# Larger reads for the MLP's first weight, a split last K pair, z1 products in the waits of z2, and the output store on another queue

## The chip, the cores and the metric

The kernel runs on one core of one Trainium2 chip. The metric is the device time of one execution in microseconds (us), lower is better. The profile's "span" of an execution is from its first to its last recorded instruction; it is 1.7 to 2.1 us shorter than the device time of the same execution in most cases, and up to 3.0 us shorter in about one of seven.

## The reference

One decode step: attention over the last 4,096 keys of 32 heads of 192, then a gated MLP. All data are bf16.

```python
# x: [1,1,640]; caches [1,32,32768,192]; wq [640,6144]; wo [6144,640]; w_in [640,1536]; w_out [768,640]
def _A_ref(x, k_cache, v_cache, wq, wo):
    q = (x @ wq) split into 32 heads
    k, v = k_cache[:, :, Sk - 4096:], v_cache[:, :, Sk - 4096:]
    p = softmax(q @ k.T * 192 ** -0.5)
    return (p @ v) @ wo
def _B_ref(x, w_in, w_sp, b_sp, w_out):
    z = gelu(x @ w_in)                    # 1,536 columns
    z1 = z[..., :768]
    z2 = layernorm(z[..., 768:])
    g = w_sp * z2 + b_sp                  # S is 1: two scalars
    return (z1 * g) @ w_out
h = x + _A_ref(layernorm(x), ...)
out = h + _B_ref(layernorm(h), ...)
```

The caches are 100.7 MB of the 119.3 MB that have to be read. w_in is 1.97 MB and w_out 0.98 MB; they are needed last, after the attention.

## The kernel before

All large loads are issued from one list by one engine (SP), in the order in which they are wanted, and wait only for buffers. Heads are worked through in 16 pairs `t`. The end of the list, and how w_in is read:

```python
win_v = B_w_in.rearrange("(c p) f -> p c f", p=P)      # c: 5 chunks of 128 rows
LAST = (0, J // 2, 3 * J // 4, 7 * J // 8, J)
def dma_pair(kind, cache, t_):                         # K or V of one head pair, 3 MB
    cuts = LAST if t_ == NP - 1 else (0, J)            # the last pair lands in four pieces
    ...
plan.append(("wo", lambda: dma_wo(NQ - 1)))
for f0 in (Fh, 0):                                     # columns 768.. (z2) first, then 0.. (z1)
    for a, b in ((0, 3), (3, DC)):
        plan.append(("w", lambda f0=f0, a=a, b=b: load(w_in_sb[:, a:b, f0:f0 + Fh], win_v[:, a:b, f0:f0 + Fh])))
for c in range(FHC):
    plan.append(("w", lambda c=c: load(w_out_sb[:, c, :], wout_v[c])))
```

So z2's half of w_in is wholly read before z1's half, in rows of 768 columns, which are packets of 1,536 bytes. The tail that consumes them:

```python
    # ... h_pc, mean and rstd2 of the layernorm of h; hb1 = h - mean
    def half_in(f0):                                   # 30 products: 5 chunks c, 6 column blocks
        zv = bank()
        for c in range(DC):
            for fb in range(FHC):
                nc.tensor.matmul(zv[:, fb:fb + 1], lhsT=w_in_sb[:, c, f0 + fb * P:...], rhs=hb1[:, c:c + 1], ...)
        return zv[:, 0:FHC]
    z2_ps = half_in(Fh)
    nc.scalar.activation(out=T3[:, 0:FHC], in_=z2_ps, func=ACT.Gelu_apprx_tanh, scale=rstd2, accum_out=sums3[:, 0:1])
    nc.vector.scalar_tensor_tensor(out=tsq[:], ...)    # the squares, and their sum
    # 16 products that put h into orow, then:
    nc.tensor.matmul(lin_ps, lhsT=rootF_f[:], rhs=sums3[:], start=True, stop=True)
    # ... VectorE and ScalarE: layernorm of z2, gz = w_sp * z2 + b_sp
    z1_ps = half_in(0)
    nc.scalar.activation(out=z1[:], in_=z1_ps, func=ACT.Gelu_apprx_tanh, scale=rstd2)
    nc.vector.tensor_tensor(out=gv[:], in0=z1[:], in1=gz[:], op=ALU.mult)
    for c in range(FHC):                               # 24 w_out products
        for g in range(NG):
            nc.tensor.matmul(orow[32 * g:32 * g + 1, :], lhsT=gv[:, c:c + 1], rhs=w_out_sb[:, c, g * OW:(g + 1) * OW], ...)
    nc.vector.tensor_copy(out=o_sb[:], in_=orow)
    nc.sync.dma_start(out=out[0, 0].rearrange("(g n) -> g n", g=NG), in_=o_sb[0::32, :])
```

Of the kernel before, what the change touches and what calls it, by code (L numbers as in the profile page):

```python
# [16 lines left out]
def kernel(  # L17
# [14 lines left out]
    nc = tc.nc  # L32
    P = nc.NUM_PARTITIONS
# [4 lines left out]
    J = W // HALF  # L38
    DC = D // P
    HD = H * Dh  # L40
    F = B_w_in.shape[-1]
    Fh = F // 2
    FC = F // P
    FHC = Fh // P
    NP = H // 2
# [10 lines left out]
    NE16 = 32  # L56

    def load(out, in_):
        eng = nc.sync
        eng.add_instruction(mybir.InstDMACopy(  # L60
            name=nc.get_next_instruction_name(), mode="Copy", queue="qSPDynamicHW",
            ins=eng.lower_ap_dma(in_, for_custom_bir_dma=True),
            outs=eng.lower_ap_dma(out, for_custom_bir_dma=True)))

    def pair_keys(cache, t, a, b):
        h0 = 4 * (t // 2) + t % 2
        k0 = Sk - W + a * HALF
        return cache[0, h0:h0 + 3:2, k0:k0 + (b - a) * HALF, :].rearrange("h (p j) d -> p h (j d)", p=HALF // 2)

    RQ = 4 * Dh // P  # L70
    NQ = NP // 2
    wo_v = A_wo.rearrange("(q e i) n -> q e (i n)", q=NQ, e=NE16)
    win_v = B_w_in.rearrange("(c p) f -> p c f", p=P)
    wout_v = B_w_out.rearrange("(c e i) n -> c e (i n)", c=FHC, e=NE16)
    wq_v = A_wq.rearrange("(c p i) n -> c p (i n)", c=DC, i=4)
    LAST = (0, J // 2, 3 * J // 4, 7 * J // 8, J)
# [15 lines left out]
    def bank():  # L92
        return psum.tile([P, 512], F32, tag="sm", name="sm_ps", bufs=3)
# [5 lines left out]
    x_row = const.tile([1, D], BF16)  # L99
    w_in_sb = wp.tile([P, DC, F], BF16)  # L100
    w_out_sb = wp.tile([P, FHC, D], BF16)

    def dma_wq(i):
        t = kvp.tile([P, KVE], BF16, tag="kv", name="wq_t")
        for c in range(2 * i, min(2 * i + 2, DC)):
            load(t[:, (c % 2) * HD:(c % 2 + 1) * HD], wq_v[c])
        tiles[("wq", i)] = t

    def dma_pair(kind, cache, t_):
        t = kvp.tile([P, KVE], BF16, tag="kv", name=kind + "_t")  # L110
        cuts = LAST if t_ == NP - 1 else (0, J)
        for a, b in zip(cuts, cuts[1:]):
            load(t[:, None, a * Dh:b * Dh], pair_keys(cache, t_, a, b))
        tiles[(kind, t_)] = t

    def dma_wo(q):
        t = wop.tile([P, RQ * D], BF16, tag="wo", name="wo_t")
        if q < NQ - 1:
            load(t[:], wo_v[q])
        else:  # L120
            rows_v = A_wo.rearrange("(q p i) n -> q p (i n)", q=NQ, p=P)[q]
            for a in range(0, RQ, RQ // 2):
                load(t[:, a * D:(a + RQ // 2) * D], rows_v[:, a * D:(a + RQ // 2) * D])
        tiles[("wo", q)] = t

    plan = [("kv", lambda i=i: dma_wq(i)) for i in range(NWQ)]
    for t_ in range(2):
        plan.append(("kv", lambda t=t_: dma_pair("k", A_k_cache, t)))
    for t_ in range(NP):
        if t_ + 2 < NP:  # L130
            plan.append(("kv", lambda t=t_ + 2: dma_pair("k", A_k_cache, t)))
        if t_ % 2 == 1 and t_ < NP - 1:
            plan.append(("wo", lambda q=t_ // 2: dma_wo(q)))
        plan.append(("kv", lambda t=t_: dma_pair("v", A_v_cache, t)))
    plan.append(("wo", lambda: dma_wo(NQ - 1)))
    for f0 in (Fh, 0):
        for a, b in ((0, 3), (3, DC)):
            plan.append(("w", lambda f0=f0, a=a, b=b: load(w_in_sb[:, a:b, f0:f0 + Fh], win_v[:, a:b, f0:f0 + Fh])))
    for c in range(FHC):
        plan.append(("w", lambda c=c: load(w_out_sb[:, c, :], wout_v[c])))  # L140
    limit = {"kv": KVB, "wo": WOB, "w": DC + FHC}
# [7 lines left out]
    def free(kind, n=1):  # L149
        live[kind] -= n  # L150
        issue()
# [10 lines left out]
    ones_bf = const.tile([P, P], BF16)  # L162
# [7 lines left out]
    rootF_f = const.tile([P, P], F32)  # L170
# [32 lines left out]
    for h_ in range(2):  # L203
        id_h = ident_f[:, 64 * h_:64 * h_ + 64].rearrange("p (g c) -> p c g", g=2)
        for k_ in range(8):
            c0 = 2 * (k_ * (h_ + 1) // 2)
# [52 lines left out]
    for gq in range(0, NQ, 4):  # L259
        for w0 in range(0, 2 * Dh, P):  # L260
            psv = sc_bank()[:].rearrange("p (q w) -> p q w", q=4)
            for c in range(DC):
                wc = wq_sb[c // 2][:, (c % 2) * HD:(c % 2 + 1) * HD].rearrange("p (q a w) -> p q a w", q=NQ, a=2)
                for a in range(2):
                    nc.tensor.matmul(psv, lhsT=xn2[:, c, a, :], rhs=wc[:, gq:gq + 4, a, w0:w0 + P],  # L265
                                     start=(c == 0 and a == 0), stop=(c == DC - 1 and a == 1))
# [9 lines left out]
    attn_ps = psum.tile([P, 512], F32, tag="acc", name="attn_ps", bufs=1)  # L276
    DH2 = D // 2
    rows = attn_ps[:, DC + 3:DC + 3 + DH2]
# [133 lines left out]
    def project(q, oT):  # L412
        wo_t = tiles.pop(("wo", q))
        o = small.tile([P, RQ], BF16, tag="o6", name="o6")
        rz = rzq.pop(q)
        if q < NQ - 1:
            o2v = oT[:, 0:2 * RQ].rearrange("p (i a) -> p a i", a=2)
            o0 = small.tile([P, RQ], F32, tag="o0", name="o0")
            nc.vector.tensor_scalar(out=o0[:], in0=o2v[:, 0], scalar1=rz[:, 0:1], scalar2=None, op0=ALU.mult)
            nc.vector.scalar_tensor_tensor(out=o[:], in0=o2v[:, 1], scalar=rz[:, 1:2], in1=o0[:], op0=ALU.mult, op1=ALU.add)  # L420
        else:
            nc.vector.tensor_scalar(out=o[:], in0=oT[:, 0:RQ], scalar1=rz[:, 0:1], scalar2=None, op0=ALU.mult)
        for i in range(RQ):
            if q < NR:
                for h_ in range(2):
                    p0 = 32 * (i % 2) + 64 * h_
                    c0 = i * D + h_ * DH2
                    nc.tensor.matmul(rows[p0:p0 + 1, :], lhsT=o[:, i:i + 1], rhs=wo_t[:, c0:c0 + DH2],  # L428
                                     start=(q == 0 and i < 2), stop=(q == NR - 1 and i >= RQ - 2))
            else:  # L430
                for nb in range(DC):
                    nc.tensor.matmul(attn_ps[:, nb:nb + 1], lhsT=wo_t[:, i * D + nb * P:i * D + (nb + 1) * P],
                                     rhs=o[:, i:i + 1], start=False,
                                     stop=(q == NQ - 1 and i == RQ - 1 and nb == DC - 1))
        free("wo")

    def fold(rows_sb):
        for c in range(DC):
            nc.tensor.matmul(attn_ps[:, c:c + 1], lhsT=x_row[0:1, c * P:(c + 1) * P], rhs=ones_bf[0:1, 0:1],
                             start=(c == 0), stop=False)  # L440
        for c in range(DC):
            for h_ in range(2):
                lo, hi = max(c * P, h_ * DH2), min((c + 1) * P, (h_ + 1) * DH2)
                if lo < hi:
                    nc.tensor.matmul(attn_ps[lo - c * P:hi - c * P, c:c + 1],
                                     lhsT=rows_sb[:, lo - h_ * DH2:hi - h_ * DH2], rhs=halfsel[:, h_:h_ + 1],
                                     start=False, stop=False)

    NR = NQ - 2
    assert NCH == 2  # L450
    for t in range(NP):
# [24 lines left out]
        if q_on:  # L476
            project((t - 5) // 2, oT)
# [22 lines left out]
    NG = 4  # L500
# [27 lines left out]
    nc.vector.tensor_tensor(out=hv2[:], in0=mh[:], in1=half_ps, op=ALU.subtract)  # L528
    rstd2 = ln_rstd(hv2)

    def half_in(f0):
        zv = bank()
        for c in range(DC):
            for fb in range(FHC):
                nc.tensor.matmul(zv[:, fb:fb + 1], lhsT=w_in_sb[:, c, f0 + fb * P:f0 + (fb + 1) * P], rhs=hb1[:, c:c + 1],
                                 start=(c == 0 and fb == 0), stop=(c == DC - 1 and fb == FHC - 1))
        return zv[:, 0:FHC]

    z2_ps = half_in(Fh)
    sums3 = const.tile([P, 2], F32)  # L540
    nc.scalar.activation(out=T3[:, 0:FHC], in_=z2_ps, func=ACT.Gelu_apprx_tanh, scale=rstd2, accum_out=sums3[:, 0:1])
    tsq = small.tile([P, FHC + 1], F32, tag="tsq", name="tsq", bufs=1)
    nc.vector.scalar_tensor_tensor(out=tsq[:], in0=T3[:], scalar=0.5 ** 0.5, in1=T3[:], op0=ALU.mult, op1=ALU.mult,
                                   accum_out=sums3[:, 1:2])
    for g in range(NG):
        for c in range(DC):
            lo, hi = max(g * OW, c * P), min((g + 1) * OW, (c + 1) * P)
            if lo < hi:
                nc.tensor.matmul(orow[32 * g:32 * g + 1, lo - g * OW:hi - g * OW], lhsT=h_pc[:, c:c + 1],
                                 rhs=ident_f[:, lo - c * P:hi - c * P], start=(lo == g * OW), stop=False)  # L550
    lin_ps = bank()[:, 0:2]
    nc.tensor.matmul(lin_ps, lhsT=rootF_f[:], rhs=sums3[:], start=True, stop=True)
    m3 = small.tile([P, 2], F32, tag="lnm", name="lnm")
    nc.vector.tensor_copy(out=m3[:], in_=lin_ps)
    hv3 = small.tile([P, 1], F32, tag="lnv", name="lnv")
# [6 lines left out]
    rstd3 = ln_rstd(hv3)  # L562
    gz = small.tile([P, FHC], F32, tag="gz", name="gz", bufs=1)
    nc.vector.tensor_scalar(out=gz[:], in0=Tw[:], scalar1=rstd3, scalar2=sp_f[:, 1:2], op0=ALU.mult, op1=ALU.add)
    z1_ps = half_in(0)
    z1 = small.tile([P, FHC], F32, tag="z1", name="z1", bufs=1)
    nc.scalar.activation(out=z1[:], in_=z1_ps, func=ACT.Gelu_apprx_tanh, scale=rstd2)
    gv = small.tile([P, FHC], BF16, tag="gv", name="gv", bufs=1)
# [1 line left out]
    for c in range(FHC):  # L570
        for g in range(NG):
            nc.tensor.matmul(orow[32 * g:32 * g + 1, :], lhsT=gv[:, c:c + 1], rhs=w_out_sb[:, c, g * OW:(g + 1) * OW],
                             start=False, stop=(c == FHC - 1))
    o_sb = small.tile([P, OW], BF16, tag="o_sb", name="o_sb", bufs=1)
    nc.vector.tensor_copy(out=o_sb[:], in_=orow)
    nc.sync.dma_start(out=out[0, 0].rearrange("(g n) -> g n", g=NG), in_=o_sb[0::32, :])

_INS = ['A_x', 'A_k_cache', 'A_v_cache', 'A_wq', 'A_wo', 'B_x', 'B_w_in', 'B_w_sp', 'B_b_sp', 'B_w_out']
_OUTS = [((1, 1, 640), 'bfloat16')]
# [24 lines left out]
```

## Time and profile before

| | before |
|---|---|
| device time, median of 6 runs | 288.17 us (287.54 to 288.41) |
| span of the profiled execution | 285.5 us |
| read | 119.34 MB, 418 GB/s over the span |
| last w_out packet has landed (packet records) | 281.72 us |
| last product starts / o_sb done / span ends | 282.18 / 282.87 / 285.5 us |

The page of before. The second and third lines cut the span into 40 slices (busy tenths of the 16 DMA engines, and what they moved); a "q" line is a DMA queue with its packets, megabytes and share of 16 engines' span; the last line sums the chain of work that ended last.

```profile
span 285.5 us, 3043 instructions
...
DMA  8999999999999999999999999999999999999992
GB/s 331 399 434 441 434 434 402 435 461 441 429 441 413 434 406 441 430 460 441 441 409 407 434 441 435 440 458 413 441 425 403 441 441 410 467 441 396 394 401 103
...
q1 hardware_dynamic: 5544, 119.35, 97.5%
q8 instruction: 9, 0.15, 0.2%
q14 instruction: 4, 0.03, 0.0%
...
DMA 67%; PE 16%; DVE 14%; SPq 1%; issue 1%; DVEq 0%
...
```

The DMA engines are busy until the last slice, and two thirds of the chain are waits for them. The row "q8 instruction" is nine packets of 16 KB with which the core fetched instructions (each is called a "fetch").

The timeline of before's tail. The columns are start (us), duration, engine, line, operation, output<-inputs, shapes and count; brackets hold idle time of the engine before the group and what ended it.

```profile
...
274.18 0.44 PEld L432 LDWEIGHTS <-wo_t 128*128 128x128 bf16 x15 [0.15 <-DMA wo_t<-in_A_wo_dram]
...
275.79 0.62 PE L535 MATMUL sm_ps<-hb_1930,w_in_sb 128*128 128x1 bf16 x18
...
276.59 0.48 PE L535 MATMUL sm_ps<-hb_1930,w_in_sb 128*128 128x1 bf16 x12 [0.18 <-DMA w_in_sb<-in_B_w_in_dram]
...
278.88 0.64 PE L535 MATMUL sm_ps<-hb_1930,w_in_sb 128*128 128x1 bf16 x18 [0.38 <-DMA w_in_sb<-in_B_w_in_dram]
...
279.82 0.48 PE L535 MATMUL sm_ps<-hb_1930,w_in_sb 128*128 128x1 bf16 x12 [0.30 <-DMA w_in_sb<-in_B_w_in_dram]
...
280.63 0.17 DVE L569 TENSOR_TENSOR gv<-z_2042,gz 128x6 bf16<-128x6 f32 x1 [0.19 <-ACT z_2042 L567]
...
280.86 1.63 PE L572 MATMUL sc_ps<-w_out_sb,gv 128*1 128x160 bf16 x24 [0.56 <-DVE gv L569]
...
282.54 0.33 DVE L575 CAST o_sb<-sc_ps 128x160 bf16<-128x160 f32 x1 [1.74 <-PE sc_ps L572]
...
```

The 18 and 12 products of L535 are z2's chunks 0 to 2 and 3 to 4, then the same for z1. The second group of z2 starts 2.41 us after the last piece of wo_t was seen (274.18 to 276.59). The 24 w_out products take 1.63 us because they wait for w_out's arrivals. The chain of waits says the same (start, duration, what):

```profile
...
264.50 12.05 DMA w_in_sb<-in_B_w_in_dram
...
276.56 5.58 DMA w_out_sb<-in_B_w_out_dram
...
282.18 0.33 PE sc_ps L572 x4
...
282.54 0.33 DVE o_sb L575
...
```

The last thing before the four last products is a DMA: when this execution ends is set by the arrival of w_out.

### The profile page before, as it was taken

The page shows a single profiled execution, that of the slowest core. Times are in us where ns is not written, and L with a number is a line of the kernel's source. Part 1 is how long each engine was busy: PE and PEld are TensorE (multiplying, and loading weights), DVE is VectorE, ACT ScalarE, POOL GpSimd, SP SyncE. Part 2 cuts the span into 40 slices and gives each one's busy share as a digit, 9 for nine tenths or more (in the row PEclk, how much of TensorE's full clock was granted, in tenths as well). Part 3 has the DMA queues.
Part 4 walks back from the last instruction along what each step waited for, and adds up shares of the span by engine and source line. Part 5 has one row for each costly group of instructions (what it writes and reads, how often), then busy time and mean ns, then how long its engine had stood idle before and what let it go on. Part 6 is the DMA issues. An engine that isn't in the chain of part 4 may idle for free.

```text
span 285.5 us, 3043 instructions
## 1 busy us (share of the span) xinstructions
PE 188.1 (66%) x1245; PEld 77.6 (27%) x1245; DVE 193.3 (68%) x282; ACT 26.4 (9%) x98; POOL 2.3 (1%) x10
## 2 busy tenths in 40 slices
PE   1229947778764665935593775756972787778873
PEld 0003413223222221312131222222321222334562
DVE  7300098989994948688595939595786849984632
ACT  2001200101102010201002010201010010202311
POOL 3000000000000000000000000000000000000000
PEclk9999989799999698979979879967797759987675
DMA  8999999999999999999999999999999999999992
GB/s 331 399 434 441 434 434 402 435 461 441 429 441 413 434 406 441 430 460 441 441 409 407 434 441 435 440 458 413 441 425 403 441 441 410 467 441 396 394 401 103
DMA packets 5563, 119.53 MB, mean 419 GB/s; under 512 B 1005, under 2 KB 2286, under 8 KB 2990
## 3 DMA queue, kind: packets, MB, share of 16 engines
q1 hardware_dynamic: 5544, 119.35, 97.5%
q8 instruction: 9, 0.15, 0.2%
q14 instruction: 4, 0.03, 0.0%
q10 hardware_dynamic: 6, 0.00, 0.0%
HBM read 119.34 MB, written 0.00 MB: 418 GB/s over the span
## 4 chain that ended last, share of the span: by engine, by line
DMA 67%; PE 16%; DVE 14%; SPq 1%; issue 1%; DVEq 0%
DMA k_t<-in_A_k_cache_dram 35%; DMA v_t<-in_A_v_cache_dram 19%; PE sc_ps L299 9%; DVE k_t L293 9%; DMA wq_t<-in_A_wq_dram 7%; PE sc_ps L265 5%; DMA w_in_sb<-in_B_w_in_dram 4%; DMA w_out_sb<-in_B_w_out_dram 2%; DVE ob L395 1%; DVE S L307 1%; SPq L60 1%; PE pv_169 L370 1%; PE attn_ps L428 1%; PE sm_ps L317 0%; DVE gm L319 0%
## 5 line engine op out<-in xcount | busy, mean ns | idle before, releaser
L299 PE MATMUL sc_ps<-k_t,ident_bf 128*128 128x512 bf16 x384 | 112.3, 455 | 43.8 <-DVE k_t L293 43.8
L293 DVE TENSOR_TENSOR k_t<-k_t,q_203 128x6144 bf16<-128x6144 bf16 x32 | 107.2, 3353 | 36.7 <-DMA k_t<-in_A_k_cache_dram 36.7
L299 PEld LDWEIGHTS <-ident_bf 128*128 128x128 bf16 x384 | 41.8, 113 | 104.6 <-issue 65.5
L265 PE MATMUL sc_ps<-wq_t,xn_128 128*128 128x512 bf16 x60 | 17.7, 455 | 10.8 <-DMA wq_t<-in_A_wq_dram 8.4
L307 DVE TENSOR_REDUCE S<-sc_ps 128x32 f32<-128x512 f32 x32 | 21.8, 682 | 2.0 <-PE sc_ps L299 2.0
L273 DVE COPY sp_f<-sm_ps 128x2 f32<-128x2 f32 x1 | 0.2, 160 | 25.9 <-PE sm_ps L271 25.9
L265 PEld LDWEIGHTS <-xn_128 128*128 128x128 bf16 x60 | 6.5, 110 | 21.6 <-issue 14.2
L332 ACT ACTIVATE E_125<-S,bias 128x64 bf16<-128x64 f32 x12 | 4.2, 360 | 73.8 <-DVE bias L326 73.8
L319 DVE TENSOR_REDUCE gm<-sm_ps 2x1 f32<-2x128 f32 x16 | 4.5, 279 | 8.4 <-PE sm_ps L317 8.4
L332 ACT ACTIVATE E_126<-S,bias 128x64 bf16<-128x64 f32 x10 | 3.5, 361 | 68.2 <-DVE bias L326 68.2
L332 ACT ACTIVATE E_127<-S,bias 128x64 bf16<-128x64 f32 x10 | 3.5, 362 | 67.1 <-DVE bias L326 67.1
L370 PE MATMUL pv_171<-v_t,E_126 128*8 128x512 bf16 (+1 forms) x72 | 7.1, 458 | 2.7 <-DMA v_t<-in_A_v_cache_dram 2.7
L370 PE MATMUL pv_169<-v_t,E_127 128*8 128x512 bf16 (+1 forms) x72 | 7.1, 457 | 0.5 <-DMA v_t<-in_A_v_cache_dram 0.5
L267 ACT ACTIVATE q_203<-sc_ps 128x512 bf16<-128x512 f32 x6 | 3.6, 597 | 29.3 <-PE sc_ps L265 29.3
L370 PE MATMUL pv_169<-v_t,E_125 128*8 128x512 bf16 (+1 forms) x72 | 6.2, 424 | 0.0
L370 PEld LDWEIGHTS <-E_126 128*8 128x8 bf16 (+1 forms) x120 | 3.4, 89 | 8.1 <-issue 5.4
L370 PEld LDWEIGHTS <-E_127 128*8 128x8 bf16 (+1 forms) x120 | 3.5, 86 | 7.1 <-issue 4.7
L370 PE MATMUL pv_171<-v_t,E_127 128*8 128x512 bf16 (+1 forms) x48 | 4.2, 425 | 1.8 <-DMA v_t<-in_A_v_cache_dram 1.8
L370 PE MATMUL pv_171<-v_t,E_125 128*8 128x512 bf16 (+1 forms) x48 | 4.2, 425 | 1.5 <-DMA v_t<-in_A_v_cache_dram 1.5
L370 PEld LDWEIGHTS <-E_125 128*8 128x8 bf16 (+1 forms) x120 | 3.2, 84 | 6.7 <-issue 4.0
L370 PE MATMUL pv_169<-v_t,E_126 128*8 128x512 bf16 (+1 forms) x48 | 4.2, 423 | 0.0
L324 PEld LDWEIGHTS sm_ps<-ident_f,gm 2*128 2x128 f32 x16 | 2.0, 128 | 7.4 <-issue 5.7
(225 smaller groups left out, 141.3 us busy)
## 6 DMA issues: line engine op xcount, KB each, us to landing
k_t<-in_A_k_cache_dram SPq DMA_DIRECT2D x15, 3072.0 KB, 32.0
v_t<-in_A_v_cache_dram SPq DMA_DIRECT2D x15, 3072.0 KB, 32.1
wq_t<-in_A_wq_dram SPq DMA_DIRECT2D x5, 1536.0 KB, 14.2
wo_t<-in_A_wo_dram SPq DMA_DIRECT2D x7, 960.0 KB, 20.5
k_t<-in_A_k_cache_dram SPq DMA_DIRECT2D x1, 1536.0 KB
v_t<-in_A_v_cache_dram SPq DMA_DIRECT2D x1, 1536.0 KB
w_in_sb<-in_B_w_in_dram SPq DMA_DIRECT2D x2, 576.0 KB, 14.0
wo_t<-in_A_wo_dram SPq DMA_DIRECT2D x2, 480.0 KB, 13.0
```

Of the source, the lines that this page charges most:

```text
L60: eng.add_instruction(mybir.InstDMACopy(name=nc.get_next_instruction_name(), mode="Copy", queue="qSPDynamicHW", ins=eng.lower_ap_dma(in_, ...
L265: nc.tensor.matmul(psv, lhsT=xn2[:, c, a, :], rhs=wc[:, gq:gq + 4, a, w0:w0 + P], start=(c == 0 and a == 0), stop=(c == DC - 1 and a == 1))
L267: nc.scalar.activation(out=q2f[:, gq:gq + 4, w0:w0 + P], in_=psv, func=ACT.Copy, scale=scale)
L293: nc.vector.tensor_tensor(out=kc, in0=kc, in1=q2[:, t:t + 1, :].to_broadcast([P, JC, Dh]), op=ALU.mult)
L299: nc.tensor.matmul(psv, lhsT=ident_bf[:], rhs=k3[:, ch * JC:(ch + 1) * JC, n * G:(n + 1) * G], start=(n == 0), stop=(n == NT - 1))
L307: nc.vector.tensor_reduce(out=S[:, ch * JC:(ch + 1) * JC], in_=st[t]["ps"][ch], axis=AX.X, op=ALU.add)
L319: nc.vector.tensor_reduce(out=gm[:], in_=mT[0:2, 0:P], axis=AX.X, op=ALU.max)
L324: nc.tensor.transpose(out=nb[:, 0:2], in_=gm[:].to_broadcast([2, P]), identity=ident_f[0:2, 0:2])
L332: nc.scalar.activation(out=E[:, :, a], in_=S[:], func=ACT.Exp, bias=bias[:, a:a + 1], accum_out=zq[q][:, a, b:b + 1])
L370: nc.tensor.matmul(pv[p0:p0 + 2 * n, :].rearrange("p (k r i) -> p k r i", k=n, r=32), lhsT=E[:, j0:j0 + n, :].rearrange("p j a -> p (j a)" ...
L395: nc.vector.tensor_reduce(out=ob[:, i0:i0 + ni], in_=flat.rearrange("p (k r i) -> p i r k", k=n, i=ni), axis=AX.X, op=ALU.add)
L428: nc.tensor.matmul(rows[p0:p0 + 1, :], lhsT=o[:, i:i + 1], rhs=wo_t[:, c0:c0 + DH2], start=(q == 0 and i < 2), stop=(q == NR - 1 and i >= ...
```

## The change

Its intent: fewer and larger packets for w_in, so that the loads end earlier; a finer last step and less work in the tail; z1's first products in time in which TensorE waits anyway; and an output store that does not use SP. Rows 0 to 383 of w_in are read whole (12,288 bytes a packet), so both halves of these rows come before z2's rows 384 to 639.

```diff
+    win_rows = B_w_in.rearrange("(c e i) f -> c e (i f)", c=DC, e=NE16)
+    WHOLE = 3
-        cuts = LAST if t_ == NP - 1 else (0, J)
+        cuts = (0, J) if t_ < NP - 1 else LAST if kind == "v" else (0, J // 2, J)
+    for c in range(WHOLE):
+        plan.append(("w", lambda c=c: load(w_in_sb[:, c, :], win_rows[c])))
     for f0 in (Fh, 0):
-        for a, b in ((0, 3), (3, DC)):
-            plan.append(("w", lambda f0=f0, a=a, b=b: load(w_in_sb[:, a:b, f0:f0 + Fh], win_v[:, a:b, f0:f0 + Fh])))
+        plan.append(("w", lambda f0=f0: load(w_in_sb[:, WHOLE:, f0:f0 + Fh], win_v[:, WHOLE:, f0:f0 + Fh])))
 ...  # x's products: 5 in the fold (the attention's rows turned into columns, near the end) become 2 in the first projection
-    z2_ps = half_in(Fh)
+    part_in(z2_ps, Fh, 0, DC)
+    part_in(z1_ps, 0, 0, WHOLE)          # z1's 18 products for rows 0 to 383
     nc.scalar.activation(out=T3[:, 0:FHC], in_=z2_ps, func=ACT.Gelu_apprx_tanh, ...)
 ...
+    nc.tensor.matmul(lin_ps, lhsT=rootF_f[:], rhs=sums3[:], start=True, stop=True)   # before h's 16 products
 ...
-    nc.tensor.matmul(lin_ps, lhsT=rootF_f[:], rhs=sums3[:], start=True, stop=True)   # was after them
 ...
-    z1_ps = half_in(0)
+    part_in(z1_ps, 0, WHOLE, DC)         # z1's other 12 products
 ...
-    nc.sync.dma_start(out=out[0, 0].rearrange("(g n) -> g n", g=NG), in_=o_sb[0::32, :])
+    nc.scalar.dma_start(out=out[0, 0].rearrange("(g n) -> g n", g=NG), in_=o_sb[0::32, :])
```

More of the change, by code (lines that the diff above doesn't have):

```diff
@@ L422, in project @@
             nc.vector.tensor_scalar(out=o[:], in0=oT[:, 0:RQ], scalar1=rz[:, 0:1], scalar2=None, op0=ALU.mult)
+        if q == 0:
+            for h_ in range(2):
+                nc.tensor.matmul(rows[64 * h_:64 * h_ + 1, :], lhsT=ones_bf[0:1, 0:1], rhs=x_row[0:1, h_ * DH2:(h_ + 1) * DH2],
+                                 start=True, stop=False)
         for i in range(RQ):
@@ L428, in project @@
                     nc.tensor.matmul(rows[p0:p0 + 1, :], lhsT=o[:, i:i + 1], rhs=wo_t[:, c0:c0 + DH2],
-                                     start=(q == 0 and i < 2), stop=(q == NR - 1 and i >= RQ - 2))
+                                     start=(q == 0 and i == 1), stop=(q == NR - 1 and i >= RQ - 2))
             else:
@@ L438, in fold @@
         for c in range(DC):
-            nc.tensor.matmul(attn_ps[:, c:c + 1], lhsT=x_row[0:1, c * P:(c + 1) * P], rhs=ones_bf[0:1, 0:1],
-                             start=(c == 0), stop=False)
-        for c in range(DC):
             for h_ in range(2):
@@ L446, in fold @@
                                      lhsT=rows_sb[:, lo - h_ * DH2:hi - h_ * DH2], rhs=halfsel[:, h_:h_ + 1],
-                                     start=False, stop=False)
+                                     start=(c == 0), stop=False)
     NR = NQ - 2
@@ L529, with part_in @@
     rstd2 = ln_rstd(hv2)
-    def half_in(f0):
-        zv = bank()
-        for c in range(DC):
+    def part_in(zv, f0, c0, c1):
+        for c in range(c0, c1):
             for fb in range(FHC):
@@ L536, in half_in @@
                                  start=(c == 0 and fb == 0), stop=(c == DC - 1 and fb == FHC - 1))
-        return zv[:, 0:FHC]
-    z2_ps = half_in(Fh)
+    z2_ps = bank()[:, 0:FHC]
+    part_in(z2_ps, Fh, 0, DC)
+    z1_ps = bank()[:, 0:FHC]
+    part_in(z1_ps, 0, 0, WHOLE)
     sums3 = const.tile([P, 2], F32)
@@ L544 @@
                                    accum_out=sums3[:, 1:2])
+    lin_ps = bank()[:, 0:2]
+    nc.tensor.matmul(lin_ps, lhsT=rootF_f[:], rhs=sums3[:], start=True, stop=True)
     for g in range(NG):
@@ L550 @@
                                  rhs=ident_f[:, lo - c * P:hi - c * P], start=(lo == g * OW), stop=False)
-    lin_ps = bank()[:, 0:2]
-    nc.tensor.matmul(lin_ps, lhsT=rootF_f[:], rhs=sums3[:], start=True, stop=True)
     m3 = small.tile([P, 2], F32, tag="lnm", name="lnm")
```

## The prediction

> **What bounds the kernel now.** DMA, to the end. The page: 119.3 MB at 418 GB/s over 285.5 us; its slice table has the DMA share at 9 tenths until the last slice; 67% of the chain of waits is DMA, its last pieces v_t (29.2 us), w_in_sb (12.1), w_out_sb (5.6). The trace's packet records show each DMA engine reading nearly without gaps from 2.1 us until it ends, between 279 and 281.7 us. After that (timeline): last w_out products 282.18 to 282.51, o_sb to 282.87, output DMA on SP (0.63 us; packets 1.2 us after the issue began), end 285.5.
>
> Close behind stands a compute chain: last z2 weights seen at 276.59, products done 277.07, gelu 277.30 (it waited for rstd2), sums, lin, layernorm, gz done 280.44, z1's gelu done 280.61, w_out products from 280.86. Those are paced by arrivals, 0.4 us per 160 KB (groups at 281.38, 281.78, 282.18). Unpaced they would need about 0.9 us (estimate, from 56 products of 192 columns in 2.41 us) and end near 281.8: some 0.7 us of slack.
>
> **What the change does, costed.**
> - w_in rows 0 to 383: 768 packets of 1,536 B become 96 of 12,288 B; packets take 65.4 and 461 ns: per engine 3.14 us become 2.77, -0.38 us. Agrees with the Trainium skill, "DMA: Bandwidth & Descriptors", "Why small descriptors are slow", which names a fixed cost per packet.
> - Last K pair: 24,576 B packets (915 ns) for 12,288 and 6,144 B ones (461, 236 ns): -0.07 us per engine.
> - So all loads end about 0.45 us earlier.
> - But z2's last weights lie behind 1.57 MB instead of 0.98: per engine 3.81 us instead of 2.62. With the K saving z2 starts 1.1 us later; 0.2 us is absorbed as gelu no longer waits for rstd2, 0.2 as gz then ends after z1's gelu. gv comes 0.8 us later.
> - z1's 18 products for rows 0 to 383 (0.64 us) fit PE's wait for gelu and sums (0.85 us): free. The other 12 end before gz. lin ahead of the h products gains nothing: it waited for tsq.
> - x products move out of the fold: off the chain.
> - Output on ACT: ACT's DMA issues took 0.21 to 0.51 us, SP's 0.63: perhaps -0.2 us. The same page, "Issuing engines are not separate DMA queues", says that another queue saves only issue time.
>
> **Sum.** DMA would allow -0.45 us, but the compute chain then ends last: +0.8 (gv) minus 0.7 (slack) is +0.1; output -0.2. Net -0.1 to -0.4 us, within the noise. The saved transfer time is mostly lost to the later z2.
>
> **Predicted:** 287.8 us, range 286.8 to 288.9 in 8 of 10. Faster by over 2%: 1%; within: 98%; slower: 1%.
>
> **What would show it.** Right: the last w_out load lands 0.4 us earlier, yet w_out products start 0.8 us later and run without the 0.4 us steps; z2's last products start near 277.7; z1's first 18 stand before lin; the chain of waits has VectorE and ScalarE between w_in_sb and the w_out products. Wrong: products still paced by w_out arrivals, or z2 no later.
>
> **What would make it wrong.** PE's instruction fetch (a 16 KB packet at 276.7 us, which slowed six neighbours on its engine to 192 ns) falls elsewhere and moves the last engine by 0.6 us. The tail's granted clock (0.5) differs. Fewer completions let SP issue earlier and close gaps that I take for zero. ACT's store is slower than SP's.

## The result, and the profile after

| | before | after |
|---|---|---|
| device time, median | 288.20 us (287.31 to 289.5, 20 runs) | 289.13 us (288.06 to 289.65, 10 runs) |
| ratio after/before | | 1.0033, 95% interval 1.0018 to 1.0047 |

A ratio is the mean time of one kernel's runs over that of the other's of the same rounds, so it is not quite the ratio of the medians. The time lies 0.2 us above the predicted range, and the sign is wrong: the change costs about 0.9 us where a gain of 0.1 to 0.4 us was expected.

The page after, the lines that answer to those of before:

```profile
span 286.3 us, 3034 instructions
...
DMA  7999999999999999999999999999999999999991
GB/s 295 433 440 433 440 426 429 418 447 433 433 428 433 440 433 440 392 462 433 440 428 427 426 440 427 424 444 440 433 414 440 433 433 412 449 440 405 398 404 62
...
q1 hardware_dynamic: 4720, 119.34, 97.1%
q8 instruction: 9, 0.15, 0.2%
...
DMA 56%; PE 21%; DVE 20%; SPq 1%; issue 1%; ACT 0%; DVEq 0%
...
```

There are 824 packets fewer on the load queue, the same nine instruction packets, and less of the chain is DMA. The timeline of its tail (12 and 6 products of L538 are z2's rows 0 to 255 and 256 to 383; the 30 are z2's last 12 and z1's first 18):

```profile
...
274.58 0.54 PE L439 MATMUL attn_ps<-o_1884,wo_t 128*128 128x1 bf16 x15 [0.27 <-DMA wo_t<-in_A_wo_dram]
...
276.40 0.46 PE L538 MATMUL sm_ps<-hb_1926,w_in_sb 128*128 128x1 bf16 x12
...
277.39 0.32 PE L538 MATMUL sm_ps<-hb_1926,w_in_sb 128*128 128x1 bf16 x6 [0.53 <-DMA w_in_sb<-in_B_w_in_dram]
...
278.33 0.96 PE L538 MATMUL sm_ps<-hb_1926,w_in_sb 128*128 128x1 bf16 x30 [0.62 <-DMA w_in_sb<-in_B_w_in_dram]
...
280.65 0.48 PE L538 MATMUL sm_ps<-hb_1926,w_in_sb 128*128 128x1 bf16 x12
...
282.09 0.17 DVE L574 TENSOR_TENSOR gv<-z_2038,gz 128x6 bf16<-128x6 f32 x1
...
282.31 0.97 PE L577 MATMUL sc_ps<-w_out_sb,gv 128*1 128x160 bf16 x24 [1.19 <-DVE gv L574]
283.33 0.33 DVE L580 CAST o_sb<-sc_ps 128x160 bf16<-128x160 f32 x1 [1.07 <-PE sc_ps L577]
...
```

And the end of its chain of waits:

```profile
...
270.36 7.92 DMA w_in_sb<-in_B_w_in_dram
...
278.33 0.49 PE sm_ps L538 x12
...
282.09 0.17 DVE gv L574
...
282.31 1.00 PE sc_ps L577 x22
...
283.33 0.33 DVE o_sb L580
...
```

The bound has moved as predicted: the last DMA in the chain is now w_in's, and after it come products, gelu, layernorm and gv. The w_out products start 1.45 us later than in before (282.31 against 280.86) but run without steps in 1.00 us, so they end only 0.80 us later (283.31 against 282.51). 0.65 us of slack was used up, where 0.7 was predicted. Yet w_out itself landed at 281.62 us, hardly earlier than before's 281.72.

Before's profile is of a fast execution (285.5 us, as short as any of its spans). In the profiles of store_only, k_only, rest_only and rest_again below, which load w_in and w_out in before's order, the w_out products start at 281.15 to 281.64 us and take 1.6 us there too. Against those the short execution of after is 0.7 to 1.2 us later, not 1.45.

One profile is one execution. The spans of all of them showed what this profile does not:

| kernel | spans of its executions, us |
|---|---|
| before, 53 executions in five sets | 285.5 to 286.7, mean 286.05 |
| after, first measurement | 286.0 286.3, then 287.3 287.3 287.3 287.3 287.3 287.4 287.4 287.4 287.6 |
| after, measured again | 286.0 286.1 286.1 286.3, then 287.5 287.7 |

After has two groups, with nothing between 286.3 and 287.3. Six of its 17 executions are short, mean 286.13, the same as before; eleven are long, mean 287.41. The mean of all is 286.96, 0.91 us or 0.32% above before's: the two groups account for the whole ratio. The profile above is of a short execution. The profile taken when after was measured again is of a long one, at 287.5 us. Its timeline:

```profile
...
277.07 0.32 PE L538 MATMUL sm_ps<-hb,w_in_sb 128*128 128x1 bf16 x6 [0.64 <-DMA w_in_sb<-in_B_w_in_dram]
...
279.55 0.96 PE L538 MATMUL sm_ps<-hb,w_in_sb 128*128 128x1 bf16 x30 [2.15 <-DMA w_in_sb<-in_B_w_in_dram]
...
283.53 0.97 PE L577 MATMUL sc_ps<-w_out_sb,gv 128*1 128x160 bf16 x24 [1.19 <-DVE gv L574]
...
```

Chunk 2 of z2 is here 0.3 us *earlier* than in the short execution, but z2's last 12 products start 2.48 us after it (279.55 less 277.07), not 0.94 us (278.33 less 277.39). Everything behind is late by the difference. What is in that gap can be read in the DMA view of the same execution, for the window 277.4 to 278.5 us:

```profile
...
q1 hardware_dynamic: 190, 0.42, 98.5%
q8 instruction: 1, 0.02, 5.8%
...
```

It holds an instruction packet. By the packet records it began at 277.45 us and took 1.01 us; five slow packets behind it end at 279.21 us, and z2's last weights have landed 0.3 us later. In the short execution a fetch is to be found at nearly the same time (277.40 us).

### What an instruction fetch does to the loads

The packet records of before have nine packets of 16,384 bytes, at 48.1, 78.3, 116.8, 146.3, 183.0, 214.4, 245.2, 269.9 and 276.7 us, of 0.88 to 1.03 us each. They follow TensorE's program: 20 more matmuls (40 instructions with their weight loads) moved the ninth from 276.7 to 275.3 us, and 192 instructions fewer moved it to 280.8 us (both below). I sorted the packets into 16 engines by letting each begin where another on the same engine ended. This is my reconstruction, not a view of the profile; it works well for the large packets and gets ambiguous among the small ones at the end. By it, a fetch keeps one engine from its loads for about 1 us, and then that engine takes 160 to 192 ns instead of 65 for each of its next five packets of 1,536 bytes. In before, between 60 and 264 us, the six engines that took a TensorE fetch fell 1.4 to 1.5 us further behind the leading engine (0.7 to 2.1, 0.6 to 2.1, 0.3 to 1.8 us for three of them). Two took a packet of the row "q14 instruction" (8,192 bytes, ScalarE's) and fell 0.6 and 0.9 us. The other eight changed by 0.1 at most. An engine that never idles does not make that up. A tile has landed when the *slowest* engine has read its part.

So the theory that the experiments test, as it stands after all of them: the ninth fetch falls into the last loads of both kernels. In before, z2's weights have just been read at 276.7 us, and the fetch holds up z1's and w_out's. It is this that paces the w_out products and makes the 0.7 us of "slack". In after, z2's last weights come over 1 us later in the list, and in most executions the held-up engine has not yet read them when the fetch comes. This is "theory C" of the expectations. The rival theories: the later z2 alone, by its order, costs the time (theory A); or other parts (the larger packets, the K pieces, the store) do (theory B).

### The profile page after: what moved, and what is told of

It reads as the page before. It is cut to its first block, busy times and chain, and to the rows that moved or that the text cites. A ratio compares the mean times of both kernels' runs of the same rounds, so it can differ in the third digit from the quotient of the medians.

```text
span 286.3 us, 3034 instructions
## 1 busy us (share of the span) xinstructions
PE 189.2 (66%) x1242; PEld 78.2 (27%) x1242; DVE 193.3 (68%) x282; ACT 26.4 (9%) x98; POOL 2.3 (1%) x10
## 4 chain that ended last, share of the span: by engine, by line
DMA 56%; PE 21%; DVE 20%; SPq 1%; issue 1%; ACT 0%; DVEq 0%
DMA k_t<-in_A_k_cache_dram 34%; DVE k_t L296 13%; DMA v_t<-in_A_v_cache_dram 13%; PE sc_ps L302 13%; DMA wq_t<-in_A_wq_dram 7%; PE sc_ps L268 5%; DMA w_in_sb<-in_B_w_in_dram 3%; DVE ob L398 2%; DVE S L310 2%; PE pv_169 L373 1%; SPq L60 1%; PE sm_ps L320 1%; PE attn_ps L435 1%; DVE gm L322 0%; PE sc_ps L577 0%
## 5 line engine op out<-in xcount | busy, mean ns | idle before, releaser
L302 PE MATMUL sc_ps<-k_t,ident_bf 128*128 128x512 bf16 x384 | 115.7, 466 | 45.2 <-DVE k_t L296 45.0
L302 PEld LDWEIGHTS <-ident_bf 128*128 128x128 bf16 x384 | 42.7, 115 | 107.9 <-issue 70.1
L268 PE MATMUL sc_ps<-wq_t,xn_128 128*128 128x512 bf16 x60 | 17.0, 441 | 11.3 <-DMA wq_t<-in_A_wq_dram 8.8
```

The source lines that it names most:

```text
L268: nc.tensor.matmul(psv, lhsT=xn2[:, c, a, :], rhs=wc[:, gq:gq + 4, a, w0:w0 + P], start=(c == 0 and a == 0), stop=(c == DC - 1 and a == 1))
L302: nc.tensor.matmul(psv, lhsT=ident_bf[:], rhs=k3[:, ch * JC:(ch + 1) * JC, n * G:(n + 1) * G], start=(n == 0), stop=(n == NT - 1))
```

## The experiments

All complete kernels below gave correct results. The four "skip" kernels leave products out: their V sums are incomplete, though they still pass the comparison. One other kernel gives a wrong result. "Before" is the kernel before in the same set on the same chip: medians 288.18, 287.85, 287.99, 288.05 and 287.95 us for sets 1 to 5. Five sets make 18 runs.

### Set 1: which part of the change costs

**win_only.** Before plus the new w_in loads, the split z1 products and lin moved; nothing else.

```diff
+    for c in range(WHOLE):
+        plan.append(("w", lambda c=c: load(w_in_sb[:, c, :], win_rows[c])))
...  # z1's first 18 products behind z2's; lin ahead of h's products
```

> The kernel before with only the w_in part of the change: rows 0 to 383 in whole rows first, z1's first 18 products and the lin product moved. Theory A (z2's weights come later and the compute chain behind them ends last): this part alone carries the loss, 1.002 to 1.0045 of before; z2's last 12 products start 1.2 to 1.8 us later after the last wo_t landing than in before, w_out products run without arrival gaps. Theory B (the loss comes from the K pieces, the x products or the store on ACT): 0.999 to 1.001.

Measured: 289.08 us, ratio 1.0022 [0.9997, 1.0047]; spans 286.0 286.2, then 287.1 287.5 287.5 287.7. The two groups are there, with the store on SP and the K pair in four pieces. In its profile, a long execution of 287.5 us, z2's chunk 2 came at 277.06 and its last products at 279.38 us, with the fetch at 277.08. The last products are 2.8 us later than in before, where 1.2 to 1.8 were expected. The ratio alone isn't clear of 1; the two groups show that the cost lies in this part.

**rest_only.** The rest of the change, with w_in read as in before.

```diff
-        cuts = LAST if t_ == NP - 1 else (0, J)
+        cuts = (0, J) if t_ < NP - 1 else LAST if kind == "v" else (0, J // 2, J)
...  # x's products in the first projection
-    nc.sync.dma_start(out=out[0, 0]...)
+    nc.scalar.dma_start(out=out[0, 0]...)
```

> The kernel before with everything else of the change: last K pair in two pieces, x products in the first projection, store from the ACT queue; w_in loads and products as before. Theory A: 0.999 to 1.001 of before, end of the store 2.6 to 2.7 us after o_sb as in before. Theory B: 1.002 to 1.0045.

Measured: 287.80 us, ratio 0.9981 [0.9965, 0.9997]; spans 285.5 to 286.2, one group. The ratio is below what was expected, but over half of the difference (0.28 of 0.52 us) lies outside the spans. The fetch came at 277.1 us here too, and the loads ended at 282.26 us, but z2's weights were already there.

**order_small.** The change with its order of loads, but with before's packets of 1,536 bytes.

```diff
-    for c in range(WHOLE):
-        plan.append(("w", lambda c=c: load(w_in_sb[:, c, :], win_rows[c])))
-    for f0 in (Fh, 0):
-        plan.append(("w", lambda f0=f0: load(w_in_sb[:, WHOLE:, f0:f0 + Fh], win_v[:, WHOLE:, f0:f0 + Fh])))
+    for a, b in ((0, WHOLE), (WHOLE, DC)):
+        for f0 in (Fh, 0):
+            plan.append(("w", lambda f0=f0, a=a, b=b: load(w_in_sb[:, a:b, f0:f0 + Fh], win_v[:, a:b, f0:f0 + Fh])))
```

> The changed kernel, but the rows 0 to 383 are read in the same order (both column halves before rows 384 to 639) in the old packets of 1,536 B. Theory A: the order is the loss and the large packets give a little of it back: z2's last products start some 0.3 to 0.4 us later than in the changed kernel, time 1.003 to 1.006 of before, above the changed kernel's 1.0033. If the large packets themselves cost (unevenness among DMA engines), it is below 1.003.

Measured: 288.49 us, ratio 1.0012 [0.9984, 1.0039]; spans 286.1 286.1 286.3, then 287.1 287.3 288.0. It missed what was expected of the time, because three of six executions were short; the profiled long one has z2's last products at 279.31 us. Two groups without large packets: the order brings them, not the packets.

**whole1.** The change with only rows 0 to 127 read whole, so that less stands ahead of z2's last weights.

```diff
-    WHOLE = 3
+    WHOLE = 1
```

> The changed kernel with only rows 0 to 127 whole (393 KB of which half belongs to z1, so z2's last weights come about 0.35 us later than in before instead of 1.2 to 1.3). Theory A: the slack of 0.7 us behind gv swallows that, 0.998 to 1.001 of before. Theory B: 1.002 to 1.0045, like the changed kernel.

Measured: 288.04 us, ratio 0.9989 [0.997, 1.0008]; spans 285.4 to 286.3, one group. z2's last products started at 277.17 us, the fetch at 277.5. With z2's weights ahead of the fetch again, the long group is gone, although a third of the large packets is kept. The order's own delay is smaller here as well, so this run doesn't tell the two apart.

### Set 2: move the fetch

**after_skip.** 96 products of early V tiles are left out, 192 TensorE instructions with their weight loads, far from the tail. The sums are incomplete.

```diff
         for j in range(lo, hi, 8):
             g = j // 8
+            if 2 <= t < 10 and 2 <= g < 6:
+                continue
```

> The changed kernel with 96 products of V tiles in the middle of the run left out (wrong result on purpose): 192 PE instructions fewer, so PE's ninth 16 KB instruction fetch, which began at 277.4 us, should come after the loads have ended. Theory C (the order explains about 1.2 us of z2's delay; in most executions the ninth fetch adds another 1.0 to 1.3 us, because it holds up one DMA engine while that still has to read z2's last weights): the two groups of spans (286.0 to 286.3 and 287.1 to 287.7) become one at or below 286.3, ratio 0.996 to 1.000 of before, z2's last products 1.2 to 1.5 us after those of c=2 at most. Theory A alone (only order): unchanged, 1.0033, two groups.

**before_skip.** The same lines in before.

```diff
+            if 2 <= t < 10 and 2 <= g < 6:
+                continue
```

> The kernel before with the same 96 products left out (wrong result on purpose). Theory C: its ninth fetch came at 276.7 us, after z2's weights were read, and only held back z1's weights and w_out; without it the last w_out load lands 0.5 to 1 us earlier and the time falls to 0.996 to 0.999 of before. If fetches cost nothing: 1.000.

Measured: after_skip 287.54 us, ratio 0.9983 [0.997, 0.9996], spans 285.6 to 285.8. before_skip 286.75 us, ratio 0.9955 [0.9943, 0.9968], spans 284.7 to 285.2. The ninth fetch now begins at 280.53 and 280.76 us, and the loads end at 280.71 and 280.90 us. The two timelines, after_skip first:

```profile
...
276.80 0.32 PE L540 MATMUL sm_ps<-hb,w_in_sb 128*128 128x1 bf16 x6 [0.63 <-DMA w_in_sb<-in_B_w_in_dram]
...
277.75 0.96 PE L540 MATMUL sm_ps<-hb,w_in_sb 128*128 128x1 bf16 x30 [0.64 <-DMA w_in_sb<-in_B_w_in_dram]
...
281.73 0.97 PE L579 MATMUL sc_ps<-w_out_sb,gv 128*1 128x160 bf16 x24 [1.18 <-DVE gv L576]
...
```

```profile
...
276.42 0.48 PE L537 MATMUL sm_ps<-hb,w_in_sb 128*128 128x1 bf16 x12 [0.18 <-DMA w_in_sb<-in_B_w_in_dram]
...
280.60 0.99 PE L574 MATMUL sc_ps<-w_out_sb,gv 128*1 128x160 bf16 x24 [1.19 <-DVE gv L571]
...
```

In after_skip z2's last products follow chunk 2 by 0.95 us, as in the short executions of after, and all its executions are of one group. In before_skip the w_out products take 0.99 us instead of 1.63: the pacing by w_out's arrivals, and with it the slack, is gone. With the fetch out of the way of both, the order costs 1.13 us at the start of the w_out products and 0.0028 of the time (0.9983 less 0.9955, 0.8 us). before_skip gained slightly more than the 0.996 to 0.999 that were expected. Two cautions: products were left out, which saves work elsewhere as well, so 0.45% for before_skip is not shown to be the fetch alone. And the eighth fetch moved too, from 269.9 (before) to 275.2 and 274.4 us; no such gap as in the long executions is seen after it, although before_plus (next) shows a ninth fetch at the same time, 275.3 us, that delays z2. What tells them apart stands at the end, under "What stays open".

**before_plus.** Before with 20 small products after the first projection, 40 instructions more.

```diff
+    idle_ps = bank()
+    for _ in range(20):
+        nc.tensor.matmul(idle_ps[:, 0:1], lhsT=ones_bf[0:1, :], rhs=ones_bf[0:1, 0:1], start=True, stop=True)
```

> The kernel before with 20 idle products added after the first projection (correct): 40 PE instructions more, so the ninth fetch starts some 1.5 us earlier, near 275 us, before z2's weights are read by every engine. Theory C: z2's last products start up to 1.3 us later than in before (276.59), 1.001 to 1.004 of before. If fetches cost nothing or only their number counts: 1.000.

Measured: 287.85 us, ratio 0.9994 [0.9981, 1.0006], spans 286.0 to 286.1. Timeline:

```profile
...
277.91 0.48 PE L538 MATMUL sm_ps<-hb,w_in_sb 128*128 128x1 bf16 x12 [1.32 <-DMA w_in_sb<-in_B_w_in_dram]
...
281.89 1.07 PE L575 MATMUL sc_ps<-w_out_sb,gv 128*1 128x160 bf16 x24 [1.15 <-DVE gv L572]
...
```

The ninth fetch came at 275.3 us, ahead of z2's last weights, and z2's last products started at 277.91 us, 1.32 us later than in before. So the late z2 can be made in the kernel *before*, with before's own order, by nothing but moving the fetch. The time did not follow: the w_out products start 1.03 us later but run unpaced in 1.1 us. In before's order the slack still takes up one fetch; expecting a slower time was a miss.

**big_z2first.** Large packets without the changed order: rest_only with w_in in packets of 6,144 bytes, z2's half first. The bytes come from wrong places of w_in, so the result is wrong (relative error 1.38).

```diff
+    flat = B_w_in.rearrange("(c u e i) f -> c u e (i f)", c=DC, u=2, e=NE16)
+    for u, f0 in enumerate((Fh, 0)):
+        for c in range(DC):
+            plan.append(("w", lambda f0=f0, c=c, u=u: load(w_in_sb[:, c, f0:f0 + Fh], flat[c, u])))
```

> The kernel of rest_only (K pieces, x products, store on ACT) with w_in read in packets of 6,144 B from the wrong places (wrong result on purpose), z2's columns first as in before: what larger packets are worth where the order is kept. Per engine 20 packets of 236 ns for 80 of 65.4 ns, 0.5 us less. Theory A and C: below rest_only's 0.9981, at 0.996 to 0.998, the last w_out load 0.5 us earlier. If large packets are themselves no gain: 0.998 or more.

Measured: 287.68 us, ratio 0.9992 [0.9979, 1.0006], spans 285.8 to 286.0. The loads ended at 282.26 us, exactly as in rest_only: a miss. The saved packet time reached neither the end of the loads nor the time. The packet records show why this is no clean test of packet size: from 274 us on, 62 of 420 packets of w_in and w_out took over a quarter longer than the median of their size, 13 us in excess of it, or 0.8 us on each of 16 engines. In rest_only none of w_out's packets did. What stretches them (the wrong places, perhaps) is not known.

### Set 3: the parts once more, and the smallest ones alone

**order_small_skip**: order_small with the V products left out as in after_skip. **rest_skip**: rest_only with the same lines.

```diff
+            if 2 <= t < 10 and 2 <= g < 6:
+                continue
```

> The order of the changed kernel in the old packets, with the 96 products left out (wrong values on purpose in few places), so without a second instruction fetch on one DMA engine. If the order costs and the large packets give back their 0.38 us, then z2's last products start 0.3 to 0.45 us later than in after_skip and the ratio is 0.0010 to 0.0016 above after_skip's 0.9983: 0.9993 to 1.0000. If packet size does not matter: 0.9983.

> rest_only (all parts but w_in) with the 96 products left out. There the compute chain behind the last V piece ends last, not the loads, so the K pieces and the store on ACT can give only what the store gives: 0.9950 to 0.9962, the same as before_skip's 0.9955 within 0.0006. If the K pieces shorten the loads and that counts: below 0.9945.

Measured: order_small_skip 287.63 us, ratio 0.9985 [0.9968, 1.0002], spans 285.6 to 286.0; z2's last products at 278.05 us, 0.30 later than in after_skip as expected, and the loads end at 280.95 us, 0.24 later, but the time is the same as after_skip's, which was a miss. rest_skip 286.43 us, ratio 0.9945 [0.9928, 0.9961], spans 284.5 to 284.9, a little below the expected 0.9950, which the interval doesn't exclude. Without the fetch, too, the order (with z1's split products and lin moved) makes a difference: 0.004 in the ratios (0.9985 against 0.9945), 1.1 us in the mean spans (285.80 against 284.68); the large packets bring 0.2 to 0.3 us in the trace and nothing that shows in the time.

**k_only** and **store_only**, each one line of the change:

```diff
-        cuts = LAST if t_ == NP - 1 else (0, J)
+        cuts = (0, J) if t_ < NP - 1 else LAST if kind == "v" else (0, J // 2, J)
```

> The kernel before with only the last K pair in two pieces. Expected from packet times: 0.07 us less per DMA engine, 0.999 to 1.000 of before. If this part is what made rest_only faster by 0.19%: 0.9970 to 0.9985.

```diff
-    nc.sync.dma_start(out=out[0, 0]...)
+    nc.scalar.dma_start(out=out[0, 0]...)
```

> The kernel before with only the store issued from ACT. The prediction said -0.2 us (0.9993). From the changed kernel's profile, where the end comes 2.6 us after o_sb on either queue: 1.000, between 0.999 and 1.001. If this part made rest_only faster: 0.9970 to 0.9985.

Measured: k_only 287.98 us, ratio 0.9992 [0.9972, 1.0012]. store_only 287.90 us, ratio 0.9999 [0.9979, 1.0019]. Neither shows a gain or a loss.

### Set 4: after again, and the fetch moved the other way

**after_again** is the changed kernel, unaltered, to see whether the groups come back and to have a second profile.

> The changed kernel once more, unaltered, for a second profile of it and its times on the chip of the next two. Theory C: if the profile falls in the group of long spans (287.0 to 287.7), z2's last 12 products start 2.0 to 2.4 us after those of c=2 (0.94 us in the first profile, of a short span of 286.3) and the ninth fetch began before z2's last weights had landed; ratio 1.002 to 1.005. If it is a short span: the fetch began after z2's last weights were read by the engine it held up, as in the first profile.

Measured: 288.08 us, ratio 1.0014 [0.9991, 1.0037]; four executions short, two long. The ratio is below the expected 1.002 to 1.005. The profile of a long one is shown above, with 2.48 us where 2.0 to 2.4 were expected. This run also shows how little six executions of a kernel with two groups say: its median is a short execution's time, that of the first measurement a long one's.

**after_plus.** The changed kernel with the 20 small products of before_plus (same diff).

> The changed kernel with 20 idle products after the first projection (correct), so 40 PE instructions more: the ninth fetch comes about 1.5 us earlier and so is always ahead of z2's last weights. Theory C: no lucky executions are left, all spans at 286.8 or above, ratio 1.003 to 1.005. Rival D (the two groups have nothing to do with when the fetch comes): again some spans at 286.0 to 286.4.

Measured: 288.98 us, ratio 1.0029 [1.0013, 1.0046]; spans 286.7 287.0 287.0 287.3 287.4 287.4: no short one is left (the least is 0.1 us under the expected 286.8). The ninth fetch came at 276.0 us, and now chunk 2 of z2 is the late one:

```profile
...
278.38 0.32 PE L541 MATMUL sm_ps<-hb,w_in_sb 128*128 128x1 bf16 x6 [1.78 <-DMA w_in_sb<-in_B_w_in_dram]
...
279.32 0.96 PE L541 MATMUL sm_ps<-hb,w_in_sb 128*128 128x1 bf16 x30 [0.62 <-DMA w_in_sb<-in_B_w_in_dram]
...
```

A ninth fetch that comes before z2's weights are read gave long executions only; one that comes after them (after_skip) gave short ones only; after's own, at 277.4 us, gives both.

**rest_again.** rest_only unaltered, because its ratio of set 1 looked like a gain.

> rest_only once more, the version that may beat both kernels, on the same chip as the changed kernel: 0.9975 to 0.9995 of before, and below the changed kernel by 0.3 to 0.6%.

Measured: 287.98 us, ratio 0.9996 [0.998, 1.0011]. The gain is not confirmed, and against the changed kernel (1.0014 here) it is 0.2%, not the expected 0.3 to 0.6. So no complete version here is shown to beat the kernel before.

### Set 5: fewer TensorE instructions in a complete kernel

**rest_act, before_act, after_act.** In each of the three kernels, 16 of 32 columns of the first half of each K tile (but the last) are summed by ScalarE instead of TensorE: 180 TensorE instructions fewer, nothing left out.

```diff
+        for j in range(lo, hi):                          # act_sums(t, 0, 8), act_sums(t, 8, 16)
+            nc.scalar.activation(out=act_out[:], in_=k3[:, j, :], func=ACT.Copy, accum_out=st[t]["S"][:, j:j + 1])
...
-        for n in range(NT):                              # 12 products over 32 columns
+        for n in range(NT // 2):                         # 6 over the other 16
```

> A complete version with fewer PE instructions: rest_only, with half of the first chunk's score sums of every K tile but the last done by ScalarE, 16 accumulating copies of 192 elements, and the other half by 6 products in place of 12: 180 PE instructions fewer. Theory C: the ninth fetch comes after the loads, as in rest_skip, though nothing is left out: 0.994 to 0.9975 of before, w_out products without arrival gaps. If ScalarE's new work delays the exponentials: 0.999 or more.

> The same ScalarE sums in the kernel before, nothing else changed. Theory C: as before_skip, 0.9945 to 0.998.

> The same ScalarE sums in the changed kernel. Theory C: one group of spans, none above 286.3, 0.997 to 1.0005, above before_act by 0.2 to 0.35%, which is what the order costs where no fetch is in the way.

Measured: rest_act 287.95 us, ratio 0.9997 [0.9984, 1.0011]; before_act 287.98 us, 1.0003 [0.999, 1.0015], spans 286.1 to 286.4; after_act 288.94 us, 1.0035 [1.0023, 1.0048], spans 286.8 to 287.2. All three missed what was expected, but after_act is above before_act by 0.32%, as expected. The ninth fetch did move to 280.8, 280.8 and 281.3 us (and the eighth into the tail, to 276.1, 275.6 and 275.8), but the last pieces of V and wo_t came about 1.2 us later than in before (wo_t at 275.39 us in before_act against 274.18), and that is what it had been hoped to gain. ScalarE now runs nearly 500 instructions more, and the page of before_act has another row grown:

```profile
...
q14 instruction: 8, 0.07, 0.1%
...
```

Before has four such packets. By the reconstruction, five of these packets (at 52, 89, 147, 194 and 249 to 250 us) fell on one and the same DMA engine, in all three kernels, and at 264 us that engine was 3.5 to 3.7 us behind the leading one; the worst engine of before was 2.2 us behind. This 1.3 us agrees with the 1.2 us by which the last V pieces are late. By this account the set traded a fetch of TensorE in the tail for fetches of ScalarE earlier. What it shows besides: after_act has one group, and with the ninth fetch behind z2's weights the order still costs 0.96 us, both at the start of the w_out products (283.12 against 282.16 us) and in the time (288.94 against 287.98).

## Why the prediction was right or wrong

**That the time stays within 2% was right; the size and the sign were not.** The range ended at 288.9 us; 289.13 were measured.

**The step that failed** is, in its words, "With the K saving z2 starts 1.1 us later" and "gv comes 0.8 us later". It was mis-sized as a term of the sum, mainly because it has no fetch in it:

| term | predicted, us | the runs |
|---|---|---|
| z2's last products, from the order of loads | +1.1 | +1.34 in the short profile (2.41 to 3.75 after wo_t), +1.33 in after_skip against before_skip |
| z2's last products, from the fetch | 0 | about +1.5 more in the long executions (2.48 us from chunk 2 instead of 0.94) |
| gv | +0.8 | +1.46 in the short profile, of which 0.4 is a later wo_t; +1.13 and +0.96 (start of the w_out products) in the pairs with the fetch out of the way; +2.68 in the long profile |
| slack of the w_out products | -0.7 | -0.65 |
| loads end | -0.45 | -0.10 in the short profile; -0.24 from the packets alone (after_skip against order_small_skip) |
| store | -0.2 | about 0 |

The sum went wrong by the second row. With about 1.0 us for gv from the order, and 1.28 us more (the distance of the groups' mean spans) in eleven of 17 executions, which is 0.83 on average, less 0.65 of slack, one gets +1.2 us; the spans show +0.91. The order's own term is a quarter larger than predicted and would have been nearly absorbed. In the short executions it was: their spans are before's.

**The fetch was named, but as the wrong kind of risk.** The prediction saw the packet at 276.7 us and said that, falling elsewhere, it "moves the last engine by 0.6 us". It took the fetch for a risk to the end of the loads. But the change itself moved z2's weights past the place where the fetch falls. The fetch hardly moved (276.7 to 277.4 us); the work moved onto it. The 0.6 us is what the slowest engine loses, and there it is not far off: without the fetch (before_skip) the loads end 0.8 us earlier. The engine that takes the fetch loses 1.4 to 1.5 us. The Trainium skill, "Runtime: NRT & Kernel Launch", "Instruction fetch mechanics", says that instructions are refilled in blocks of 16 KiB (256 instructions) by the sequencer's own DMA queue, which agrees with TensorE's nine packets of 16,384 bytes and with the way that they moved; ScalarE's packets (q14) have 8,192 bytes. It calls the cost of crossing such a boundary "one DMA tail-bump, mostly hidden". Whether TensorE itself ever waited for it was not looked at; it was not hidden from saturated loads, and here the measurement decides.

**The slack was right in size, and had another cause than I thought.** I took it for a property of w_out's packets. In before_skip, where the fetch falls at the end of the loads, the w_out products are not paced (0.99 us for 24), although the loads are the same. The slack and the later z2 are two forms of one fetch: before pays for it in w_out's arrivals, after in z2's.

**Smaller packets of time.** That a larger packet costs less per byte is confirmed: 65.4 ns for 1,536 bytes and 461 for 12,288 is 62 ns saved on eight, or 9 ns for each packet avoided, which agrees with a fixed cost per packet as in the Trainium skill, "DMA: Bandwidth & Descriptors", "Why small descriptors are slow". The saving of 0.4 us per engine came out as 0.24 us at the end of the loads where only the packets differ (order_small_skip against after_skip), and as 0.10 in the first pair of profiles. Part of the -0.10 is a later start: the page's first slice has 295 GB/s instead of 331, and wo_t, which has nothing to do with w_in, came 0.4 us later. None of it shows in the time, as the loads' end is no longer what ends last.

**Right:** the w_out products lose their 0.4 us steps, 18 products of z1 run in a wait and cost nothing, VectorE and ScalarE enter the chain, moving lin ahead and x's products out of the fold changes nothing that shows (neither was tested alone). **The store** gains nothing: from the end of o_sb to the end of the span are 2.67 us in before (282.87 to 285.54) and 2.62 after (283.66 to 286.28), and store_only is at 0.9999. That agrees with the same page, "Issuing engines are not separate DMA queues", which says that only the time of issuing is saved; that was 0.63 us on SP and 0.61 on ACT.

**What stays open.** What decides on which of the 16 engines a fetch falls. The packet records, sorted again by a stricter rule (each engine has to read the known sequence of packet sizes), give a part of the answer. In nine traces (before, store_only, k_only, rest_only, rest_again, before_plus, order_small, after_again, after_plus) the first eight fetches fell on eight different engines and the ninth on the engine that had taken the first. As the ninth ended, this engine was 2.8 to 3.3 us behind the leading one and all others 2.5 at most; only in the profile of before, where it had been among the first to start reading, was it 2.4 behind. In the short profile of after no engine was more than 2.6 us behind then. In the four skip kernels the eighth fetch (274.4 to 275.2 us) fell on an engine that had taken none and left it 0.9 to 1.7 us behind, less than the slowest. So by this reconstruction it is a *second* fetch on an engine that is already late that holds up a tile.

Only one short execution of a kernel with two groups was profiled, and three long ones of unaltered fetch (after_again, win_only, order_small). In the three, counted back from the landing at 65 ns a packet, the engine that took the fetch still had 9 to 13 of its 16 packets of z2's last weights to read; without the fetch it would have ended with the slowest. In the short one all must have been read on the fetch's engine before it came, since z2's products start at 278.33 us, as the fetch ends. Both counts rest on the reconstruction where it is weakest. That a short execution is one whose fetch falls on an engine further ahead fits all runs and the sorting above, but with one short profile it is inferred. The gain of before_skip and rest_skip (0.45 and 0.55%) is not shown to come from the fetch alone.

## What to carry to other kernels

In a kernel that is bound by DMA to its end, look up where the instruction packets fall in the last loads, and keep what the longest compute chain needs ahead of them; a reordering of the last loads has to be costed against the packets that it moves past, not by its bytes alone. Look at the spans of all executions before explaining one profile: two groups in them are a finding, and a profile of the other group tells another story. A slack that is read from a profile can be the mark of a disturbance, so ask what makes it before spending it.

## What the Trainium skill lacked or had wrong

- "Runtime: NRT & Kernel Launch", "Instruction fetch mechanics", has fetches mostly hidden. With the loads saturated they were not: TensorE's 16,384 bytes took 0.88 to 1.03 us of one DMA engine (before), that engine fell back by 1.4 to 1.5 us in all, and z2's last weights came 2.3 to 2.5 us after the chunk before them instead of 0.94 (win_only, after_again). It gives blocks of 16 KiB; ScalarE's packets had 8,192 bytes.
- No page says that the packets *behind* a fetch are slower too: 1,536 bytes took 160 to 192 ns instead of 65 for five packets (before).
- "DMA: Bandwidth & Descriptors" does not say that a lag of one of the 16 engines persists as long as none idles: start lags of 0 to 1 us and fetch lags of 1.4 to 1.5 us were both still there up to 200 us later (my reconstruction from packet records).
- No page warns that moving work to ScalarE brings fetches of its own: ScalarE's instruction packets went from four to eight with nearly 500 instructions more, five fell on one DMA engine, and it was 3.5 us behind the leading one at 264 us.
